# A fused Fourier-mixing and feed-forward kernel: six of seven output sums with second-level products, and a batch held in quarters

## Chip, cores and metric

The kernel runs on one core of one Trainium2 chip. The metric is the device time of one execution in microseconds. The core has five engines that each work through a queue of their own in order: TensorE (PE, with weight loads shown as PEld), VectorE (DVE), ScalarE (ACT), GpSimd (POOL) and SyncE (SP), which here issues transfers. Semaphores make an instruction of one queue wait for an instruction of another. PE writes its results into PSUM, which has 8 banks of 512 fp32 values per partition; the other tiles lie in SBUF.

## The reference

```python
def _attn_ref(x):                      # x: (8, 3008, 256) fp32
    X = np.fft.fft(x, axis=1)
    X = np.fft.fft(X, axis=2)
    return X.real.astype(np.float32)

def _moe_ref(x, w_in, w_out):          # x: (24064, 256), w_in: (256, 2048), w_out: (2048, 256)
    h = x @ w_in
    g = h * (1.0 / (1.0 + np.exp(-1.702 * h)))
    return (g @ w_out).astype(np.float32)
```

All arrays are fp32. The real part of a two-dimensional Fourier transform of each of the 8 batches goes, row by row, through two matrix products with a sigmoid-weighted activation between them.

## The kernel before

**Two pipelines in one.** The transform along the sequence (3008 = 47 x 64) is done per batch in two stages. Stage one folds the rows of `x` in the tile `xt` on GpSimd (`fold1`, 16 parts per batch), multiplies them by cosine and sine tables on PE (`mix1`, 4 times per batch, L233), copies the result back to `xt` on ACT (`mixed`) and spills it to DRAM (`spill`). Stage two reads it back (`fill`), fixes one column (`rotate`), and per block makes the tile `pq` with 32 small pairs of matmuls and four VectorE transposes (`stage2`, L354, three blocks per batch). The transform along the 256 channels is folded into the first weight matrix (`wcs`).

**Steps.** The feed-forward part runs in 384 steps: 8 batches x 3 blocks x 2 halves `hh` x 8 steps `p`. A step handles 256 hidden units (two groups of 128) for a group of 256 columns, or 226 in the second half of a first block. Eight steps with `p` from 0 to 7 are a group: they add up one output tile. The step loop (L989 to L1082) writes all engines' work out by hand, in the order in which each engine is to do it; nothing reorders it later. Extra work (folds, transforms, transfers) hangs on step numbers in the table `extra`. `paced` is a one-word transfer that holds SP's queue until a given step.

**One step t** (t from 8 on). `begin(t, 0)` and `begin(t, 1)` multiply the two parts of `pq` by `wcs` into a PSUM bank `x` (two banks, taken in turn); `middle(t)` has put a rank-one term there before, on ACT. Between the two, ACT copies twice the half-finished sum away (`doubled`). `begin(t, 1)` stands at the head of step t, `begin(t+1, 0)` in the middle of it. From the finished bank, `forward(t)` (ACT, L607) makes the activation of the forward rows, `backward(t)` (VectorE, L565) the values of the mirrored rows, and `activate_back(t)` (ACT, L614) their activation. So there are four operand tiles: A11, A12 (forward) and A21, A22 (backward).

**Seven products.** The second matrix product is done by a Strassen-Winograd scheme on these four tiles: seven products instead of eight, with sums S1 to S4 of the operands. GpSimd makes S1 and S3 (L622, L623); VectorE makes S2 and S4 for two steps at a time (L629, L630). The products of step t are issued three steps later (`LAG` = 3). Three of them (with A11, S2, S3) are plain products, 256 columns wide, into the banks `o0` and `o1` (`product`). The other four (A12, S4, A22, S1; two pairs) use a second level of the same scheme over two steps: VectorE makes four more sums (`deeper`, L651, 512 wide) and PE seven half-size products for each of the four (`small_products`, L685, 128 columns, k = 1 to 7), into the tile `low` of three banks, with k = 1 in `o1`. The weight sums for them are made once (`small_weights`).

**A group's end.** Three steps after a group's last step ACT copies two results out of PSUM (L754, L756) and VectorE adds others (L757, L758); in the step after that `combine_small` reads `low` in four additions (L786), `swap` moves halves between partitions on ACT in three copies, `combine_last` adds (L768, L804), and `turn_last` transposes the tile on VectorE in two halves, each of which is stored in DRAM by SP.

```python
            if t < n:
                backward(t)
            if t + 1 < n:
                doubled(t + 1)
            if t < n:
                activate_back(t)
                sums(t, nc.gpsimd)
```

Of the kernel before, what the change touches and what calls it, by code (L numbers as in the profile page):

```python
# [27 lines left out]
F32 = mybir.dt.float32  # L28
# [84 lines left out]
def kernel(ctx: ExitStack, tc, x, w_in, w_out, tab1, tab2, out):  # L113
# [6 lines left out]
    NCH = 8  # L120

    const = ctx.enter_context(tc.tile_pool(name="const", bufs=1, space=SB))
    xp = ctx.enter_context(tc.tile_pool(name="xp", bufs=1, space=SB))
    tp = ctx.enter_context(tc.tile_pool(name="tp", bufs=1, space=SB))
# [26 lines left out]
    o_banks = [psp.tile([128, 512], F32, tag=f"o{i}", name=f"o{i}") for i in range(2)]  # L151
    rest = psu.enter_context(tc.tile_pool(name="psu", bufs=1, space=PS))
    big = cv.tile([128, 19 * 1024], F32, tag="big", name="big")
# [13 lines left out]
    spare = ["b0", "b1", "b2", "o2", "o3", "o4"]  # L167
# [19 lines left out]
    xt = xp.tile([128, NJ, D], F32, tag="x", name="xt")  # L187
# [11 lines left out]
    def load_x(b, k):  # L199

        r, (p0, p1) = k // 2, PIECES[k % 2]
        t, src = xt[64 * r + p0:64 * r + p1], x[b].rearrange("(p j) d -> p j d", j=NB)[p0:p1]
        pairs = [4 * D, 8], [1, 2 * D]
        for lo, rows_, at in ((0, src, 2 * r), (16, Xr[b][p0:p1], 2 - 2 * r)):
            nc.sync.dma_start(out=t[:, lo:lo + 16, :].rearrange("p (i c) d -> p i (c d)", c=2),
                              in_=free(rows_, at * D, *pairs))
# [3 lines left out]
    def fold1(b, c, part, eng):  # L210

        t = xt[0:64 + NA]
        if c == 0 and part == 0:

            e, t0 = cv.tile([NA, 2, D], F32, tag="e", name="e"), xt[0:NA]
            e0[b] = e
            fwd, rev = free(t0, 1, [31 * D, 2], [1, H - 1]), free(t0, D - 1, [31 * D, 2], [-1, H - 1])
            eng.tensor_tensor(e[:, :, 1:H], fwd, rev, op=ALU.add)
            eng.tensor_copy(free(e[:], 0, [D, 2], [H, 2]), free(t0, 0, [31 * D, 2], [H, 2]))
            eng.tensor_tensor(e[:, :, H + 1:D], fwd, rev, op=ALU.subtract)  # L220

        at, up = 2 * c * D, (31 - 2 * c) * D
# [10 lines left out]
    def mix1(b, m):  # L233
# [3 lines left out]
        for i in (2 * m, 2 * m + 1):  # L237
            for r in range(2):
                for c in range(2):
                    rows, o = slice(64 * r, 64 * r + NA), ps[r][64 * c:64 * c + 64, i % 2 * D:(i % 2 + 1) * D]  # L240
                    jj, todo = 4 * i + 2 * r + c, queues.setdefault((r, c), [])
                    if jj:
                        todo.append((2, o, mat(w1, jj, rows), xt[rows, 31 - (2 * i + c), :], not todo, True))
                        continue
# [17 lines left out]
    def mixed(m, r, ps):  # L262
        nc.scalar.copy(free(xt[:], (4 * m + r) * D, [2 * D, 2], [1, D]), free(ps[:], 0, [D, 2], [1, D]))
# [73 lines left out]
    def spill(b, c, q):  # L337

        nc.sync.dma_start(out=view(Td[b], (16 * c + 4 * q) * D, [NJ * D, NM], [1, 4 * D]),
                          in_=xt[64 * c:64 * c + NM, 4 * q:4 * q + 4, :].rearrange("p q d -> p (q d)"))  # L340

    def fill(b, a0=0, a1=NG):
        if a0 == 0:
            t4t[b] = tp.tile([128, NG, D], F32, tag="t4", name="t4")
        nc.sync.dma_start(out=t4t[b][:, a0:a1, :], in_=Td[b].rearrange("(a p) d -> p a d", p=128)[:, a0:a1, :])

    def rotate(b, a0=0, a1=NG, copy=None):

        col = t4t[b][:, a0:a1, H]
        ps = bank("psr")  # L350
        halves(ps[:, 0:a1 - a0], rot, col, start=True, stop=True)
        (copy or nc.vector.tensor_copy)(col, ps[:, 0:a1 - a0])

    def stage2(b, blk):  # L354

        pq, t4 = pqp.tile([128, 2, 512], F32, tag="pq", name="pq"), t4t[b]
# [3 lines left out]
        for cs in range(2):  # L360
            for h in range(2):
                for g in range(4):
                    for u in range(NU):
                        rows, at = slice(64 * u, 64 * u + 64), cs * 256 + h * 128
                        nc.tensor.matmul(ps[u][32 * g:32 * g + 32, at:at + 128], lhsT=m[rows, cs, h * RUN:(h + 1) * RUN],  # L365
                                         rhs=t4[rows, 4 * blk:4 * blk + 4, cs * H + 32 * g:cs * H + 32 * g + 32],
# [23 lines left out]
    def paced(t):  # L390
        nc.sync.dma_start(out=Tk[t:t + 1, :], in_=big[0:1, at_left(t, A11):at_left(t, A11) + 1])
# [118 lines left out]
    LEFT, MADE, RIGHT, SUM, RES, OUT = 0, 4096, 8192, 14336, 16384, 18432  # L510
    A11, A21, S3, S2 = range(4)
    A12, S4, A22, S1 = range(4)
# [26 lines left out]
    def at_left(t, q):  # L539
        return LEFT + t % 4 * 1024 + q * 256  # L540

    def at_right(t, q):
        return RIGHT + (t // 2 % 3 * 2 + t % 2) * 1024 + q * 256

    def left(t, q, n):
        return big[:, at_left(t, q):at_left(t, q) + n]
# [3 lines left out]

    def front(t):
        at = at_left(t, A11)
        return free(big[:], at, [at_right(t, A12) - at, 2], [1, width(t)])

    def back(t):
        at = at_left(t, A21)
        return free(big[:], at, [at_right(t, A22) - at, 2], [1, width(t)])
# [51 lines left out]
    def backward(t):  # L609
        at = at_left(t, A21)  # L610
        reversed_sum(big[:, at:at + 256], at_right(t, A22) - at, gt.pop(t), xb.pop(t), width(t), ALU.subtract)

    def activate_back(t):
        nc.scalar.activation(back(t), back(t), ACTF.Gelu_apprx_sigmoid)  # L614

    def sums(t, eng):

        if not NP <= t < len(steps):
            return
        n = width(t)  # L620
        if eng is nc.gpsimd:
            eng.tensor_tensor(right(t, S1, n), left(t, A21, n), right(t, A22, n), op=ALU.add)  # L622
            eng.tensor_tensor(left(t, S3, n), left(t, A11, n), left(t, A21, n), op=ALU.subtract)  # L623
            return
        if t % 2 == 0:
            return
        a11, s2 = (free(big[:], at_left(t - 1, q), [1024, 2], [1, n]) for q in (A11, S2))
        a12, s4, s1 = (free(big[:], at_right(t - 1, q), [1024, 2], [1, n]) for q in (A12, S4, S1))
        eng.tensor_tensor(s2, s1, a11, op=ALU.subtract)  # L629
        eng.tensor_tensor(s4, a12, s2, op=ALU.subtract)  # L630
# [5 lines left out]
    def raws(t, half):  # L636

        return free(big[:], at_right(t, 0) + half * (width(t) // 2), [256, 4], [1, width(t) // 2])

    def made_sum(q, w):  # L640
        return free(big[:], SUM + 512 * q, [128, 4], [1, w])

    def deeper(t, part):
# [5 lines left out]
        for out, i0, i1, how in (((s3, a11, a21, ALU.subtract), (s1, a21, a22, ALU.add), (s2, s1, a11, ALU.subtract)),  # L649
                                 ((s4, a12, s2, ALU.subtract),))[part]:  # L650
            nc.vector.tensor_tensor(out, i0, i1, op=how)  # L651

    SPOT = {2: 0, 6: 1, 5: 2, 7: 3, 3: 4, 4: 5}

    def spot(pair_, k):
        return 256 + 128 * pair_ if k == 1 else 768 * pair_ + 128 * SPOT[k]

    def both(k, *dims):
        return free((o_banks[1] if k == 1 else pot["low"])[:], spot(0, k), [spot(1, k) - spot(0, k), 2], *dims)

    def small_products(t, ks):

        if t < 0 or not deep(t) or not steps[t][3] % 2:
            return
        p, w = steps[t][3] - 1, width(t) // 2
        for k in ks:
            for pr in range(2):
                for side in range(2):
                    op_ = 2 * pr + side
                    weights, q = ((wo, 2), (wo, 3), (wt, 2), (wt, 3))[op_]  # L670
                    y0, y1 = (weights[:, p + i, q, :] for i in range(2))
                    at = MADE + (p // 2 * 2 + pr) * 512 + side * 64
                    lhs = {1: y0[:, 0:64], 2: y1[:, 0:64], 3: y1[:, 64:128]}.get(k)
                    if lhs is None:
                        at += {5: 0, 6: 1, 7: 2, 4: 3}[k] * 128
                        lhs = big[:, at:at + 64]
                    raw_ = {1: (t - 1, 0), 2: (t, 0), 4: (t, 1)}.get(k)
                    if raw_:
                        rhs = right(raw_[0], op_, 256)[:, raw_[1] * w:raw_[1] * w + w]
                    else:  # L680
                        i0 = SUM + 512 * {5: 0, 6: 1, 7: 2, 3: 3}[k] + 128 * op_
                        rhs = big[:, i0:i0 + w]
                    first_in = p == 0 and (k, pr) in ((2, 0), (2, 1), (4, 1))
                    o = (o_banks[1] if k == 1 else pot["low"])[64 * side:64 * side + 64, spot(pr, k):spot(pr, k) + w]
                    nc.tensor.matmul(o, lhsT=lhs, rhs=rhs, start=first_in, stop=(p == NP - 2), skip_group_check=True)  # L685

    def small_weights(n):

        def y(i, at):
            return free(wot[:], (2 * n + i) * 4 * H + 2 * H + at, [NF // 2 * 4 * H, 2], [H, 2], [1, 64])  # L690

        b11, b12, b21, b22 = y(0, 0), y(0, 64), y(1, 0), y(1, 64)
        t1, t2, t3, t4 = (free(big[:], MADE + n * 1024 + q * 128, [512, 2], [64, 2], [1, 64]) for q in range(4))
        for out, i0, i1 in (t1, b12, b11), (t2, b22, t1), (t3, b22, b12), (t4, b21, t2):
            nc.vector.tensor_tensor(out, i0, i1, op=ALU.subtract)

    def product(t, lo, hi):

        p, n = steps[t][3], width(t)
        if lo == 0 and p == 0:  # L700
            for q in range(2):
                pot[q] = bank(f"po{q}", f"o{q}")
            if t >= NP:
                pot[2] = pot["low"]
            if t >= last:
                pot[3] = bank("po3", "b2")
        if t < NP:

            h = ht[t]
            plan = [(half, dh, wo[:, p, 2 * f + dh, :], h[:, half, f, :n])  # L710
# [400 lines left out]
```

## Time and profile before

| what | value |
|---|---|
| runs | 1854.57, 1854.43 and 1856.62 us; median 1854.57 |
| profiled execution | 1853.1 us from its first to its last instruction (its time by the clock of the runs is not given apart) |
| PE busy | 1836.6 us, 99% |
| VectorE busy | 1520.9 us, 82% |
| ACT busy | 1150.5 us, 62% |
| GpSimd busy | 975.2 us, 53% |
| granted TensorE clock | 0.999 |
| HBM | 64.41 MB read, 48.05 MB written, 61 GB/s |

The profile is of one execution. "Busy" is the share of the span in which an engine worked on at least one instruction, so overlapping instructions count once. The line numbers in profiles are those of the kernel that was profiled. Every fp32 matmul is recorded twice, and products come in pairs (two halves of 64 output rows), so four records make one pair.

### The profile page before, as it was taken

The page shows a single profiled execution, that of the slowest core. Times are in us where ns is not written, and L with a number is a line of the kernel's source. Part 1 is how long each engine was busy: PE and PEld are TensorE (multiplying, and loading weights), DVE is VectorE, ACT ScalarE, POOL GpSimd, SP SyncE. Part 2 cuts the span into 40 slices and gives each one's busy share as a digit, 9 for nine tenths or more (in the row PEclk, how much of TensorE's full clock was granted, in tenths as well). Part 3 has the DMA queues.
Part 4 walks back from the last instruction along what each step waited for, and adds up shares of the span by engine and source line. Part 5 has one row for each costly group of instructions (what it writes and reads, how often), then busy time and mean ns, then how long its engine had stood idle before and what let it go on. Part 6 is the DMA issues. An engine that isn't in the chain of part 4 may idle for free.

```text
span 1853.1 us, 56093 instructions
## 1 busy us (share of the span) xinstructions
PE 1836.6 (99%) x23722; PEld 1401.3 (76%) x23722; DVE 1520.9 (82%) x2222; ACT 1150.5 (62%) x2241; POOL 975.2 (53%) x1053
## 2 busy tenths in 40 slices
PE   8999999999999999999999999999999999999998
PEld 4677777777777777777777777777777777778776
DVE  6988778887798778987789878888888888878874
ACT  5666656665666666666566666666665666656663
POOL 4776446744368434773348643485445754444442
PEclk9999999999999999999999999999999999999999
DMA  8721340215012240223302132121411111100111
GB/s 280 181 61 34 85 67 19 72 52 99 19 46 48 73 81 13 52 50 90 57 13 67 43 86 52 19 75 35 103 31 23 37 46 36 31 19 13 23 19 24
DMA packets 149707, 105.31 MB, mean 57 GB/s; under 512 B 106057, under 2 KB 130665, under 8 KB 148896
## 3 DMA queue, kind: packets, MB, share of 16 engines
q1 hardware_dynamic: 146624, 99.68, 23.6%
q8 instruction: 187, 3.06, 0.7%
q10 hardware_dynamic: 2832, 2.05, 0.5%
q14 instruction: 64, 0.52, 0.1%
HBM read 64.41 MB, written 48.05 MB: 61 GB/s over the span
## 4 chain that ended last, share of the span: by engine, by line
PE 80%; DVE 9%; POOL 4%; ACT 2%; DMA 2%; issue 2%; SPq 0%; DVEq 0%; ACTq 0%; POOLq 0%
PE x L184 29%; PE o L184 22%; PE low L685 21%; PE o L685 3%; DVE big L651 3%; PE ps L255 2%; DVE big L786 2%; DVE big L565 1%; PE ps L365 1%; POOL xt L227 1%; DVE big L629 1%; POOL big L623 1%; DMA xt<-in_x_dram 1%; ACT big L607 1%; DMA Td<-big 1%
## 5 line engine op out<-in xcount | busy, mean ns | idle before, releaser
L622 POOL TENSOR_TENSOR big<-big 128x256 f32<-128x256 f32 (+1 forms) x376 | 353.0, 939 | 825.1 <-ACT big L614 691.4
L184 PE MATMUL x<-pq,wcs 128*64 128x256 f32 (+1 forms) x6016 | 768.8, 376 | 2.0 <-ACT g L604 1.4
L651 DVE TENSOR_TENSOR big<-big 128x512 f32<-128x512 f32 (+1 forms) x736 | 623.1, 861 | 23.4 <-PE low L685 4.7
L184 PE MATMUL o<-big,wo 128*64 128x256 f32 (+1 forms) x4800 | 620.8, 375 | 0.1
L184 PEld LDWEIGHTS x<-pq,wcs 128*64 128x64 f32 x6016 | 412.3, 137 | 186.0 <-issue 15.0
L184 PEld LDWEIGHTS o<-big,wo 128*64 128x64 f32 x4800 | 341.6, 137 | 148.0 <-DVE big L629 0.5
L604 ACT ACTIVATE g<-x 128x512 f32<-128x512 f32 (+1 forms) x376 | 221.6, 589 | 366.3 <-PE x L184 365.0
L565 DVE TENSOR_TENSOR big<-g,x 128x512 f32<-128x512 f32 (+2 forms) x440 | 254.1, 589 | 209.4 <-ACT big L607 209.0
L592 ACT ACTIVATE x<-nb,af 128x256 f32<-128x256 f32 (+1 forms) x752 | 352.9, 469 | 79.7 <-DVE pq L371 63.6
L685 PE MATMUL low<-big 128*64 128x128 f32 (+1 forms) x5888 | 382.8, 270 | 0.0
L685 PEld LDWEIGHTS low<-big 128*64 128x64 f32 x5888 | 337.5, 137 | 29.2
L623 POOL TENSOR_TENSOR big<-big 128x256 f32<-128x256 f32 (+1 forms) x376 | 352.6, 938 | 0.0
L607 ACT ACTIVATE big<-x 128x512 f32<-128x512 f32 (+1 forms) x376 | 219.2, 583 | 127.5 <-PE x L184 121.3
L614 ACT ACTIVATE big<-big 128x512 f32<-128x512 f32 (+1 forms) x376 | 231.9, 617 | 46.0 <-DVE big L565 44.0
L685 PE MATMUL low<-big,wo 128*64 128x128 f32 (+1 forms) x2944 | 220.4, 271 | 0.1
L685 PEld LDWEIGHTS low<-big,wo 128*64 128x64 f32 x2944 | 171.3, 137 | 4.2 <-DVE big L651 1.4
L630 DVE TENSOR_TENSOR big<-big 128x512 f32<-128x512 f32 (+1 forms) x188 | 160.8, 855 | 6.5
L629 DVE TENSOR_TENSOR big<-big 128x512 f32<-128x512 f32 (+1 forms) x188 | 137.3, 730 | 5.3 <-POOL big L622 5.3
L786 DVE TENSOR_TENSOR big<-big,low 128x512 f32<-128x512 f32 (+3 forms) x184 | 109.0, 609 | 3.5
L685 PEld LDWEIGHTS o<-big,wo 128*64 128x64 f32 x1472 | 92.2, 137 | 25.0
L685 PE MATMUL o<-big,wo 128*64 128x128 f32 (+1 forms) x1472 | 110.0, 270 | 0.0
L227 POOL TENSOR_TENSOR xt<-xt 111x510 f32<-111x510 f32 x56 | 86.0, 1535 | 4.4
(95 smaller groups left out, 966.2 us busy)
## 6 DMA issues: line engine op xcount, KB each, us to landing
out_dram<-os SPq DMA_DIRECT2D x284, 64.0 KB
t<-Td SPq DMA_DIRECT2D x22, 512.0 KB
Td<-xt SPq DMA_DIRECT2D x56, 192.0 KB
xt<-in_x_dram SPq DMA_DIRECT2D x14, 512.0 KB
xt<-Xr SPq DMA_DIRECT2D x14, 512.0 KB
nb<-Nd SPq DMA_DIRECT2D x23, 256.0 KB
out_dram<-os SPq DMA_DIRECT2D x96, 56.0 KB
Xr<-in_x_dram SPq DMA_DIRECT2D x7, 752.0 KB
```

What stands on the lines that cost most here:

```text
L184: nc.tensor.matmul(out[c0:c0 + 64], lhsT=lhs[:, c0:c0 + 64], rhs=rhs, skip_group_check=True, **how)
L565: nc.vector.tensor_tensor(free(out, at + m - 1, [by, 2], [RUN, blocks], [-1, m]), *ins, op=op)
L592: nc.scalar.activation(x[:, i * 256:i * 256 + n], nbt[b, blk][:, hh * 256:hh * 256 + n], ACTF.Copy, scale=af1[:, f:f + 1])
L604: nc.scalar.activation(two(g[:], n), two(xb[t][:], n), ACTF.Copy, scale=2.0)
L607: nc.scalar.activation(front(t), two(xb[t][:], width(t)), ACTF.Gelu_apprx_sigmoid)
L614: nc.scalar.activation(back(t), back(t), ACTF.Gelu_apprx_sigmoid)
L622: eng.tensor_tensor(right(t, S1, n), left(t, A21, n), right(t, A22, n), op=ALU.add)
L623: eng.tensor_tensor(left(t, S3, n), left(t, A11, n), left(t, A21, n), op=ALU.subtract)
L629: eng.tensor_tensor(s2, s1, a11, op=ALU.subtract)
L630: eng.tensor_tensor(s4, a12, s2, op=ALU.subtract)
L651: nc.vector.tensor_tensor(out, i0, i1, op=how)
L685: nc.tensor.matmul(o, lhsT=lhs, rhs=rhs, start=first_in, stop=(p == NP - 2), skip_group_check=True)
```

## The change

- Six of the seven operands (A12, S4, A22, S1, S2, S3: three pairs) now go through the second level; only A11 keeps a plain product. `deeper` works on 768 columns, `small_product` has three pairs, `small_weights` makes more weight sums.
- All output sums lie in one tile `low` of six PSUM banks; `o0`, `o1` and the bank `b2` are given up, so the transforms take both `x` banks. A step with a transform issues products of two steps around it, and the step after it none of its own. Products wait in a list `pending`, from which `issue(n)` takes about n ns of them.
- A21 is written back into the `x` bank (ACT), and S3 and S1 are made on VectorE from there, S2 and S4 on GpSimd.
- The batch in transformation is held in two quarters of 8 columns (`xq`, inside the tile `big`) in place of the whole `xt`; loads, folds, `mix1` and spills follow quarter by quarter, spread over a batch's steps. `t4` is held per block, and `rotate` is done per block.
- `combine`, `swap`, `combine_last` and `turn_last` are re-timed; `doubled(t+1)` stands behind `activate_back(t)`.

```diff
-    LEFT, MADE, RIGHT, SUM, RES, OUT = 0, 4096, 8192, 14336, 16384, 18432
+    LEFT, SUM, MADE, RIGHT, RES, TMP, MADE2, KEPT, OUT = 0, 1024, 4096, 8192, 17408, 18944, 19456, 21504, 23040
+    A12, S4, A22, S1, S2, S3 = range(6)
...
+    def activate_back(t, there):
+        n = width(t)
+        x = xb.pop(t)
+        a21[t] = x[:, 0:n] if there else turned_rows(t, n)
+        nc.scalar.activation(a21[t], turned_rows(t, n), ACTF.Gelu_apprx_sigmoid)
+        nc.scalar.activation(right(t, A22, n), right(t, A22, n), ACTF.Gelu_apprx_sigmoid)
+
+    def sums(t):
+        n, a = width(t), a21.pop(t)
+        nc.vector.tensor_tensor(right(t, S3, n), left(t, n), a, op=ALU.subtract)
+        nc.vector.tensor_tensor(right(t, S1, n), a, right(t, A22, n), op=ALU.add)
+        nc.gpsimd.tensor_tensor(right(t, S2, n), right(t, S1, n), left(t, n), op=ALU.subtract)
+        nc.gpsimd.tensor_tensor(right(t, S4, n), right(t, A12, n), right(t, S2, n), op=ALU.subtract)
...
     def made_sum(q, w):
-        return free(big[:], SUM + 512 * q, [128, 4], [1, w])
+        return free(big[:], SUM + 768 * q, [128, 6], [1, w])
...
+    SPOT = {1: 0, 2: 1, 6: 2, 5: 3, 7: 4, 3: 5, 4: 6}
+    PAIRS = 3
     def spot(pair_, k):
-        return 256 + 128 * pair_ if k == 1 else 768 * pair_ + 128 * SPOT[k]
+        return 256 + 384 * SPOT[k] + 128 * pair_
...
+    def units(t):
...
+        todo += [(436, product, t, *it) for it in plan(t)]
+        if t >= NP and p % 2 and deep(t):
+            now = [(222, small_product, t, k, pr) for k in (1, 2, 4, 7) for pr in range(PAIRS)]
+        if t > NP and p % 2 == 0 and deep(t - 1):
+            late = [(222, small_product, t - 1, k, pr) for k in (5, 6, 3) for pr in range(PAIRS)]
+        return late + todo + now if p == 0 else todo + late + now
...
         if deep(t):
-            nc.scalar.copy(free(big[:], RES + 1024 + 384, [512, 2], [1, n // 2]), both(1, [1, n // 2]))
+            nc.scalar.copy(free(big[:], KEPT + 384, [512, PAIRS], [1, n // 2]), both(1, [1, n // 2]))
+            return
...
+            now, after, soon = (k in special for k in (t, t - 1, t + 1))
+            if now and special[t][0] is stage2:
+                spare[:] = [f"b{(t + 1) % 2}"]
+                rotate(*special[t][1])
+            if t < n:
+                begin(t, 1)
...
+                forward(t)
+            combine(t - LAG - 1)
+            if t == NP + LAG:
+                psu.close()
+                low = ctx.enter_context(tc.tile_pool(name="low", bufs=1, space=PS))
+                pot["low"] = low.tile([128, 6 * 512], F32, tag="low", name="low")
+            if not after:
+                pending += units(t - LAG)
+            if now:
+                backward(t)
+                activate_back(t, False)
+                issue(1750)
+                deeper(t - 2, 0)
+                deeper(t - 3, 2)
+                sums(t)
+                transform(t)
+                deeper(t - 2, 1)
+                deeper(t - 3, 3)
+                pending += units(t + 1 - LAG)
+                issue(2100 if special[t][0] is stage2 else 1800)
+                begin(t + 1)
+                doubled(t + 1)
+                middle(t + 2)
+                issue(880)
+            else:
+                issue(0 if after else 1100)
+                if t + 1 < n:
+                    begin(t + 1)
+                held = [pending.pop() for _ in range(5)][::-1] if t - LAG == last else []
+                issue()
+                if t < n:
+                    backward(t)
+                    activate_back(t, True)
+                if t + 1 < n:
+                    doubled(t + 1)
+                deeper(t - 2, 0)
+                deeper(t - 3, 2)
+                if t < n:
+                    sums(t)
+                if t + 2 < n and not soon:
+                    middle(t + 2)
+                combine_small(t - LAG - 1)
+                pending += held
+                issue()
+                deeper(t - 2, 1)
+                deeper(t - 3, 3)
```

## The prediction

> **What bounds the kernel now.** I read the page's first two parts, then the busy table of one plain group of eight steps, the groups by shape, and the timeline around a group's end. The page:
> ```profile
> span 1853.1 us, 56093 instructions
> PE 1836.6 (99%) x23722; PEld 1401.3 (76%) x23722; DVE 1520.9 (82%) x2222; ACT 1150.5 (62%) x2241; POOL 975.2 (53%) x1053
> PEclk9999999999999999999999999999999999999999
> ```
> TensorE is busy 99% at full clock. The table from 203.07 to 239.47 us, eight steps without a transform (time; PE, PEld, DVE, ACT, POOL busy):
> ```profile
> 203.07:239.47 36.40, 36.40 (x508) 28.30 (x504) 29.32 (x45) 21.71 (x42) 15.43 (x16) 1.00 0.45 90
> ```
> PE never pauses, VectorE has 7 us left. The timeline where a group ends (start, length):
> ```profile
> 286.30 0.39 PE L685 MATMUL low<-big,wo 128*64 128x128 f32 x4
> 286.73 2.46 DVE L786 TENSOR_TENSOR big<-big,low 128x512 f32<-128x512 f32 x4
> 287.38 1.46 PE L184 MATMUL o<-big,wo 128*64 128x256 f32 x12
> 288.67 1.03 PE L184 MATMUL x<-pq,wcs 128*64 128x256 f32 x8
> ...
> 292.13 0.61 PE L685 MATMUL low<-big,wo 128*64 128x128 f32 x8
> 292.57 1.04 PE L685 MATMUL low<-big 128*64 128x128 f32 x16
> ```
> Two things are to be seen. Four records are one pair of halves: x12 against x8 gives 0.43 us per 256-column pair, x16 against x8 0.215 per 128-column pair (8 x 7 x (0.43 + 0.215) = 36.1, against 36.40). And VectorE reads `low` for 2.46 us from 0.04 us after its last product, while PE next writes `low` 5.4 us later: covered.
>
> The shapes that price the new work (mean ns behind the bar):
> ```profile
> L607 ACT ACTIVATE big<-x 128x512 f32<-128x512 f32 x312 | 184.7, 592 | 109.1 <-PE x L184 103.4 <-POOL big L623 3.1 <-DMA out_dram<-os 0.6
> L565 DVE TENSOR_TENSOR big<-g,x 128x512 f32<-128x512 f32 x312 | 210.7, 675 | 192.9 <-ACT big L607 192.7
> L804 DVE TENSOR_TENSOR big<-big 128x768 f32<-128x768 f32 x38 | 36.7, 966 | 3.9
> L786 DVE TENSOR_TENSOR big<-big,low 128x256 f32<-128x256 f32 x38 | 15.7, 414 | 0.0
> L754 ACT COPY big<-o 128x256 f32<-128x256 f32 x39 | 14.2, 365 | 5.7 <-PE o L184 5.7
> L592 ACT ACTIVATE x<-nb,af 128x256 f32<-128x256 f32 x624 | 295.3, 473 | 50.8 <-DVE pq L371 40.0
> ```
> The second says that `backward` waits for `forward`. How fast PE resumes after ACT:
> ```profile
> 368.00 0.60 ACT L604 ACTIVATE g<-x 128x512 f32<-128x512 f32 x1
> 368.65 0.65 PE L184 MATMUL x<-pq,wcs 128*64 128x256 f32 x4 [0.24 <-ACT g L604]
> ```
> That is 0.05 us. An engine's next start lies closer than the mean length: L604 to L614 0.50 (287.65 and 288.15), L754 to L756 0.27, the 768-wide L804 to L565 0.88.
>
> **Products.** A deep step had 7 pairs of each size; it gets 5 wide and 10.5 narrow ones. That is 2 x 0.43 - 3.5 x 0.215 = 0.11 us less, 0.86 a group; the table's 36.40 would have 0.22 for a narrow pair and 0.72. I take 0.8: for 46 groups, 8 of them 226 wide, **-36** (32 to 39). It is all on PE, so on the path. Rotating per block adds 15 pairs of tiny matmuls at 0.1 to 0.2: **+2**.
>
> **First wait at a group's end.** `low` now holds all sums. In the program as built, 46 times, in the step where p is 3 (three behind the group's last), the first product after `begin(t,1)` waits for ACT's copy of the k=1 sums, though it writes other columns. ACT must first do `forward(t)`, which waits for that same `begin`. From the first matmul of `begin`: its records end at 1.03, ACT starts 0.11 later, 0.50 to the copy of c11, 0.27 to the 384-wide copy, whose length between the 365 (256 wide) and the 592 (512 wide) is 0.48, then 0.05: 2.44. PE would have gone on at 0.86. Lost: 1.58.
>
> **Second wait.** The first of the four `combine_small` additions waits for the new group's opening product, the last of that step. The next product, after the next `begin`, waits for the last addition; every later product stands behind it in PE's queue. The product's end trails its issue by 0.17, VectorE starts 0.04 later; 0.88 + 0.88 + 0.47 + 0.97 = 3.20 (the 384-wide between the 414 and the 687 of the 256- and 512-wide L786); 0.05 to PE. `begin` covers 0.86. Lost: 0.17 + 0.04 + 3.20 + 0.05 - 0.86 = 2.60. VectorE is free by then: its `S1` ends at about 4.0 (`backward` starts at 1.77; 0.61, 0.88, 0.33, 0.41) and the opening product at 5.9 (2.44, nine narrow pairs, a `begin`, a product, 0.17).
> Together 4.18 a group, about 3.8 in the 226-wide: 38 x 4.18 + 8 x 3.8 = **+189**. Bounds by the rows: the 384-wide copy 0.37 to 0.60, the additions 2.46 (as before) to 3.9 (four of 966): 3.3 to 5.0 a group, 152 to 225; the middle, for the 768 row is the very shape.
>
> [...] The built program waits, so I count it.
>
> **Steps after a transform.** There are 50 (28 `mix1`, 22 `stage2`). The transforming step takes products of two steps, so its successor has two `begin`s and 4 (`stage2`) or 5 (`mix1`) narrow pairs: 2.58 or 2.80 us of PE. `doubled(t+1)`, for which the following `begin` waits, now stands on ACT behind both `activate_back`s, and they wait for `backward`: 1.03 + 0.11 + 0.59 + 0.03 + 0.68 + 0.03 + first activation 0.27 to 0.41 (L754, L592) + second 0.27 + doubled 0.60 + 0.05 = 3.66 to 3.80. Lost: 22 x 1.15 + 28 x 0.93 = **+51** (30 to 65). Plain steps last 4.1 to 4.8 and cover the chain. Two short stops per batch around `mix1` (0.50 and 0.24 in the timeline) fall into this: **-3** (-5 to 0).
>
> **VectorE and GpSimd.** By start to start, VectorE has per step `backward` 0.61, S3 and S1 0.33 each, two 768-wide sums 1.75, and per group 6.5 of combining: 3.83 a step against 3.1 before. S1 and S3 take A21 from PSUM: like L565 they should not be slowed by GpSimd, while sums with two SBUF inputs are (L651 averages 857 for 512 columns, about 680 without GpSimd beside). At up to 0.6 of that VectorE needs 4.4 of PE's 4.45: cover is thin without the waits, but with them a step averages over 5 us. **0** (up to +10); late sums would stop PE in the short steps first. GpSimd's two sums run behind S1 and are needed a step later: nothing.
>
> **Transfers.** Loads go from 56 DMAs to 224, markers from 63 to 91, on SP's queue between stores and spills. That queue waited 885 us for `os`, so it has room; 32 added issues per batch at 0.3 to 1.6 lie beside PE. A quarter is asked for two steps (9 us) before its first fold. If it came late, that fold, and GpSimd's sums queued behind it, would wait, and PE after a step's slack. **0** (0 to +10). Spills and fills keep five steps to `stage2`.
>
> **Head.** `small_weights` issues 8 VectorE additions for 4, about 1.1 us in each of four steps (PE was short of work there: steps of 5.8 and 7.1); and `low` takes over the o-banks at step 11, behind two transposes: **+4** (0 to 8). The tail is one loop pass longer, with no PE work in it.
>
> **Sum**: 1853 - 36 + 2 + 189 + 51 - 3 + 4 = 2060 of span; the runs' median lies 1.5 above the span: **2062**, 11% slower. 0.2% is about what a measurement of this kernel can tell from no change.
>
> **Rivals.**
> *PE stays the bound*: the waits are met early, and only the products count. 1853 - 36 + 2 + 4 + 1.5 = 1825. For it: TensorE's 99%. Against: the additions alone last 3.2 us behind 0.86 of cover; it decides where PE idles under 0.8 us a group; I count 5.2.
> *Only the steps after a transform stall*: the group's end is covered by something that I count as serial, as it was before (5.4 us against 2.46). 1825 + 48 = 1873. Against: both waits stand between neighbours in PE's queue.
> *VectorE too*: PE idles as forecast and VectorE, kept waiting for the opening product, cannot catch up, so the following steps each lose some 0.6 to GpSimd: up to 46 x 2 = 92 more, 2150. Against: 34 us of VectorE in groups of 42.
> *The clock falls* in the new pauses. No row here shows it: the longest pause in mid-kernel is 0.51 and the clock 0.999.
> [...]
>
> **Numbers.** Forecast 85%, from 2020 (waits and after-steps at their lower ends, 37 + 21 less, not both in full) to 2105 (the upper ends in part). Faster rival 4%, the 1873 one 5%, the two above 6%. The 2 in 10 that may be left out are the rivals and the forecast's own tails, so the range stays 2020 to 2105. Faster 0.05, same 0.01, slower 0.94.
>
> **What would show it.** Right: PE's busy share near 88%; 46 pauses of about 1.4 before a narrow `low` product released by ACT's 384-wide copy, 46 of about 2.4 before a wide one released by `combine_small`; 50 of about 1 before an `x` matmul released by `doubled`; PE's busy sum some 30 us lower. Wrong: `low` products that start while those additions run, VectorE busy over 95%, or a clock below 0.95.

## The result, and the profile after

The changed kernel takes 2250.05 us (median of 4 runs, 2237.58 to 2256.38) against 1854.57: 1.2119 times the time before [1.2083, 1.2156]. The forecast was 2062 (2020 to 2105). The sign was right; the loss is 396 us where 207 were forecast. The profiled execution has a span of 2254.6 us and a mean TensorE clock of 0.966.

The page of the changed kernel: span, then busy time, share and instructions by engine, and the clock by slice:

```profile
span 2254.6 us, 61518 instructions
PE 1940.9 (86%) x25990; PEld 1508.5 (67%) x25990; DVE 1665.0 (74%) x2629; ACT 1245.4 (55%) x2617; POOL 1005.8 (45%) x1053
PEclk9999999999999999999999999999999999999999
```

TensorE stands 314 us, and its busy share comes close to the one that I named (86 for 88%). That is chance: the forecast had some 257 us of standing and 1803 us of work, and both are too low. TensorE's busy time is 104 us more than before, though the products became less work. For the larger part that is the sign of slower matmuls, which a row of forty slices rounded to tenths does not show. The waits, summed by the waiting engine and its releaser (total us, times, longest):

```profile
PE low L185 <- DVE big L802: 121.1, 46, 3.5
PE low L681 <- ACT big L773: 64.0, 46, 1.7
PE x L185 <- ACT g L602: 58.1, 74, 3.1
PE ps L255 <- DVE big L563: 29.3, 26, 2.0
PE psr L185 <- DVE big L625: 10.2, 15, 1.0
PE ps L364 <- DVE t L351: 6.3, 14, 0.6
```

The first three are forecast: both waits at `low`, and `x` behind `doubled` (L602). The last three, about 50 us with what lies beside them, stand inside transforms and were forecast at nothing. A group's end, as the timeline of the changed kernel shows it (start, length, what ended the idle time before):

```profile
526.67 0.60 ACT L605 ACTIVATE big<-x 128x512 f32<-128x512 f32 x1 [0.90 <-PE x L185]
527.16 0.37 ACT L771 COPY big<-low 128x256 f32<-128x256 f32 x1
527.41 0.50 ACT L773 COPY big<-low 128x384 f32<-128x384 f32 x1
527.96 1.31 PE L681 MATMUL low<-big 128*64 128x128 f32 x20 [1.40 <-ACT big L773]
...
531.49 3.40 DVE L802 TENSOR_TENSOR big<-big,low 128x768 f32<-128x768 f32 x4 [1.97 <-PE low L185]
...
534.94 0.65 PE L185 MATMUL low<-big,wo 128*64 128x256 f32 x4 [2.64 <-DVE big L802]
536.08 1.84 PE L185 MATMUL x<-pq,wcs 128*64 128x256 f32 x8
```

The pauses of 1.40 and 2.64 are the two that were worked out. The last line was not: eight `x` matmuls of 1.03 us take 1.84, for the clock stands at 0.50 from 536.16 us on; the twelve 128-wide ones that follow take 1.50, against 0.82 at 530.19. Two stretches around a transform show it plainly (window; its length; PE, PEld, DVE, ACT, POOL busy; clock; DMA share, GB/s):

```profile
505.50:508.90 3.40, 1.61 (x24) 0.99 (x20) 3.33 (x5) 0.00 (x0) 1.92 (x2) 0.99 0.00 0
508.90:515.70 6.80, 6.54 (x46) 4.57 (x48) 4.72 (x7) 2.78 (x6) 2.70 (x2) 0.50 0.13 23
```

In the first stretch TensorE is busy 1.61 of 3.40 us, with no pause over 2.04; in the 6.8 us that follow it works almost throughout and the clock stands at 0.50. The trace has 41 such half-clock stretches, 153.7 us together, so some 77 us of TensorE's time, half of that, are lost (5.4 and 3 in the kernel before). About 25 follow the second pause at a group's end, ten lie in steps that transform.

### The profile page after: what moved, and what is told of

It is laid out like the page before. It is cut to its first block, busy times and chain, and to the rows that moved or that the text cites. A ratio compares the mean times of both kernels' runs of the same rounds, so it can differ in the third digit from the quotient of the medians.

```text
span 2254.6 us, 61518 instructions
## 1 busy us (share of the span) xinstructions
PE 1940.9 (86%) x25990; PEld 1508.5 (67%) x25990; DVE 1665.0 (74%) x2629; ACT 1245.4 (55%) x2617; POOL 1005.8 (45%) x1053
## 3 DMA queue, kind: packets, MB, share of 16 engines
q10 hardware_dynamic: 2832, 2.05, 0.4%
## 5 line engine op out<-in xcount | busy, mean ns | idle before, releaser
L648 DVE TENSOR_TENSOR big<-big 128x768 f32<-128x768 f32 (+1 forms) x736 | 733.7, 997 | 0.0
L681 PE MATMUL low<-big 128*64 128x128 f32 (+1 forms) x8832 | 588.9, 276 | 64.0 <-ACT big L773 64.0
L681 PEld LDWEIGHTS low<-big 128*64 128x64 f32 x8832 | 516.6, 140 | 144.1 <-ACT big L773 84.5
L563 DVE TENSOR_TENSOR big<-g,x 128x512 f32<-128x512 f32 (+2 forms) x440 | 257.4, 597 | 463.5 <-ACT big L605 461.2
L681 PE MATMUL low<-big,wo 128*64 128x128 f32 (+1 forms) x6624 | 460.8, 278 | 0.0
L681 PEld LDWEIGHTS low<-big,wo 128*64 128x64 f32 x6624 | 400.8, 141 | 55.9 <-issue 12.4
L185 PE MATMUL low<-big,wo 128*64 128x256 f32 (+1 forms) x1696 | 255.1, 390 | 122.6 <-DVE big L802 121.1
L616 ACT ACTIVATE x<-big 128x256 f32<-128x256 f32 (+1 forms) x326 | 125.1, 384 | 361.6 <-DVE big L563 358.3
L602 ACT ACTIVATE g<-x 128x512 f32<-128x512 f32 (+1 forms) x376 | 217.2, 578 | 172.4 <-PE x L185 171.2
L185 PEld LDWEIGHTS low<-big,wo 128*64 128x64 f32 x1696 | 117.0, 140 | 183.1 <-DVE big L802 141.7
L802 DVE TENSOR_TENSOR big<-big,low 128x768 f32<-128x768 f32 (+2 forms) x184 | 151.1, 838 | 89.7 <-PE low L185 86.3
L617 ACT ACTIVATE big<-big 128x256 f32<-128x256 f32 (+1 forms) x376 | 149.0, 396 | 0.0
L624 DVE TENSOR_TENSOR big<-big,x 128x256 f32<-128x256 f32 (+1 forms) x326 | 132.7, 407 | 3.7 <-ACT x L616 3.7
L625 DVE TENSOR_TENSOR big<-x,big 128x256 f32<-128x256 f32 (+1 forms) x326 | 133.8, 410 | 0.0
L616 ACT ACTIVATE big<-big 128x256 f32<-128x256 f32 (+1 forms) x50 | 20.7, 414 | 106.3 <-DVE big L563 106.3
```

The lines of the kernel that those rows point to most:

```text
L185: nc.tensor.matmul(out[c0:c0 + 64], lhsT=lhs[:, c0:c0 + 64], rhs=rhs, skip_group_check=True, **how)
L563: nc.vector.tensor_tensor(free(out, at + m - 1, [by, 2], [RUN, blocks], [-1, m]), *ins, op=op)
L602: nc.scalar.activation(two(g[:], n), two(xb[t][:], n), ACTF.Copy, scale=2.0)
L616: nc.scalar.activation(a21[t], turned_rows(t, n), ACTF.Gelu_apprx_sigmoid)
L617: nc.scalar.activation(right(t, A22, n), right(t, A22, n), ACTF.Gelu_apprx_sigmoid)
L681: nc.tensor.matmul(pot["low"][64 * side:64 * side + 64, at:at + w], lhsT=lhs, rhs=rhs, start=first_in, stop=(p == NP - 2), skip_group_chec ...
```

## The experiments

Each time is the median of 4 runs; the ratio, with its interval, is to the kernel before, run on the same chip. The kernel before took 1854.6 to 1856.5 us on these chips, so the times of different experiments can be compared; the changed kernel's own four runs spread over 19 us. Pauses are TensorE's idle times of over 0.1 us, from 80 us on, in the profiled run, summed by the tile that it writes next: `x`, `low`, and `ps` and `psr` inside transforms.

**The order on ScalarE, turned back.**

```diff
                     backward(t)
-                    activate_back(t, True)
                 if t + 1 < n:
                     doubled(t + 1)
+                if t < n:
+                    activate_back(t, True)
```

> The changed kernel with one order turned back: in steps without a transform, ScalarE issues doubled(t+1) ahead of activate_back(t), as the kernel before had it. The changed kernel's trace has 62.3 us of TensorE pauses before an x matmul (82 of them), put down mostly to ScalarE's g; the term of the forecast for them was 51. Theory (the order on ScalarE makes them): these pauses fall under 15 us, PE's other pauses stay as they are, and the time falls by 45 to 60 us, to about 2195 of 2250. Rival (the order is not the cause: backward, or the product before it, is late anyway): the time stays within 10 us and the pauses move to the next product.

Measured: 2295.94 us, 1.2376 [1.2347, 1.2405], 46 slower. Theory and rival both fell. The `x` pauses did drop, from 62 to 21 us, but the others grew: `low` from 187 to 210, transforms from 50 to 92; half clock from 154 to 201 us. A group's end of this kernel:

```profile
535.73 0.60 ACT L602 ACTIVATE g<-x 128x512 f32<-128x512 f32 x1 [2.33 <-PE x L185]
536.23 0.38 ACT L616 ACTIVATE x<-big 128x256 f32<-128x256 f32 x1
536.64 0.42 DVE L624 TENSOR_TENSOR big<-big,x 128x256 f32<-128x256 f32 x1 [2.21 <-ACT x L616]
537.31 3.39 DVE L802 TENSOR_TENSOR big<-big,low 128x768 f32<-128x768 f32 x4
540.75 0.65 PE L185 MATMUL low<-big,wo 128*64 128x256 f32 x4 [2.96 <-DVE big L802]
```

ScalarE now stands at `doubled` (L602) for TensorE, with `activate_back` (L616) behind it; VectorE waits 2.21 for that, and the additions, for which TensorE waits, start later: 2.96 in place of 2.64. The larger growth, 42 us, lies inside transforms. There too TensorE waits for VectorE's `backward` (L563), and that comes later. The transform whose matmuls wait 2.04 us in the changed kernel (shown further down) waits here:

```profile
515.44 1.97 PE L255 MATMUL ps<-big,w 47*64 47x256 f32 x12 [2.97 <-DVE big L563]
```

**The second wait, then both, taken away.** The additions of `combine_small` read SBUF (`kept` is a region of `big`); in the second kernel the two copies do too.

```diff
-        for out, i0, i1 in ((res(RES, KEPT - RES), res(KEPT + 384, 0), both(2, [384, 2], [1, w])),
+        for out, i0, i1 in ((res(RES, KEPT - RES), res(KEPT + 384, 0), kept(2, [384, 2], [1, w])),
...
-        nc.scalar.copy(c11, pot[0][:, 0:n])
+        nc.scalar.copy(c11, big[:, MADE:MADE + n] if deep(t) else pot[0][:, 0:n])
```

> The changed kernel, in which the four additions of combine_small read a fixed region of SBUF in place of low; left out is the use of the sums that low holds. The additions stay, of the same shapes; nothing but the copies at the first wait now reads low at a group's end. The second wait goes: 46 pauses, 122.6 us of TensorE idle time. Theory A (the wait and the clock): idle time falls by 110 to 130 us, and of the 41 stretches at half clock the 30 or so that follow the second pause go too, another 45 to 60 us of slow matmuls: 2250 - 170 = about 2080 (2065 to 2095). Theory B (idle time alone; the half clock comes from elsewhere and stays): 2250 - 125 = about 2125, with about 40 half-clock stretches left. Theory C (VectorE is behind, and its lateness comes back at the next wait): less than 60 us gained.

> As the run before it in this list, and in addition the copies of c11 and of the k=1 sums by ScalarE read SBUF at a group's end: nothing reads low there (left out: all use of the deep sums). Both waits go. Against the run with the second wait alone taken away: theory A, the first wait was a cost of its own, and 46 x 1.39 = 64 us go, to about 2015. Rival: the pause only moves to the x matmuls behind it, for ScalarE's forward ends the same step, and less than 25 us go. If the forecast's other terms hold, what is left over the 1825 of my first rival is then the steps after a transform (62), the transform waits (50) and what clock is lost there.

Measured: 2167.33 us, 1.168 [1.1652, 1.1707], and 2167.91 us, 1.1677 [1.1657, 1.1696]. Two pauses worth 187 us of TensorE gave 82, less than theories A and B and more than C, and the first of them gave nothing, as its rival had it: the `x` pauses grew from 62 to 126 and 178 us. Half clock fell from 154 to 57 us and, without the first wait, rose to 131 again. The kernel without either wait, at a group's end:

```profile
2046.84 4.23 DVE L805 TENSOR_TENSOR big<-big 128x768 f32<-128x768 f32 x4
...
2051.85 0.68 DVE L563 TENSOR_TENSOR big<-g,x 128x512 f32<-128x512 f32 x1
2052.56 0.39 ACT L616 ACTIVATE x<-big 128x256 f32<-128x256 f32 x1 [3.77 <-DVE big L563]
...
2053.19 0.58 ACT L602 ACTIVATE g<-x 128x512 f32<-128x512 f32 x1
2053.82 1.08 PE L185 MATMUL x<-pq,wcs 128*64 128x256 f32 x8 [1.82 <-ACT g L602]
```

The additions hold up `backward` (L563) behind them, that ScalarE, that TensorE. The edit also lengthens them, 3.40 to 4.23 us, for both inputs now lie in SBUF; so these two runs understate the waits.

**The clock by itself.** Products with zero weights fill the two pauses.

```diff
+                for lag, pairs in ((1, 3), (2, 5)):
+                    if t + 1 < n and group_end(t - LAG - lag):
+                        idle(t + 1, pairs)
                 issue(0 if after else 1100)
```

> The changed kernel with zero-weight products in the two pauses at each group's end: 3 pairs of 64-row halves, 256 columns wide, where the first pause is (1.3 of 1.39 us), 5 pairs where the second is (2.15 of 2.64 us). They add zero to the x bank just written, so nothing of the result changes, and TensorE has 46 x 3.4 = 157 us more to do. Theory (the clock follows how busy TensorE was in the stretch before): of the 41 half-clock stretches 153.7 us long in all, the 30 behind the second pause go, and the time FALLS by 35 to 60 us though work is added, to about 2200. Rival (the clock is no cause; pauses are just time): the products fit into the pauses or overrun them, and the time stays or rises by up to 40 us. The mean clock of the profiled run tells: 0.966 now; by the theory 0.985 or more.

Measured: 2207.96 us, 1.1898 [1.188, 1.1916], 42 faster with 101 us more on TensorE (PE busy 2041.8 for 1940.9). Half clock fell from 153.7 to 36.3 us, which gives back 59, and the mean clock rose from 0.966 to 0.992, as the theory had it; the rest went into overrunning the pauses. The rival, that pauses are just time, falls.

**VectorE's additions, late sums and the order, left out one upon another.** From the kernel without reads of `low`:

```diff
-                combine_small(t - LAG - 1)
+                if t < 4 * NP:
+                    combine_small(t - LAG - 1)
...
-            combine_last(t - LAG - 5, 0)
+            if t < 4 * NP:
+                combine_last(t - LAG - 5, 0)
```

> As the kernel in which nothing reads low at a group's end, and in addition the four additions of combine_small are left out behind all but the first two deep groups (their sums are not made). Theory (VectorE's 3.4 us in one piece set the step they stand in, whatever PE waits for by name: backward, S3 and S1 of the next step are queued behind them, and with backward, activate_back, doubled and the next begin): without them the step that lasted 7.1 us falls to 4.8 or less, x pauses of 178 us to under 90, and with them half of the half-clock stretches: 44 x 2.3 = 100 and 30 to 50 of clock off 2167, so about 2030 (2000 to 2070). Rival (VectorE has slack there, and the pauses come from ScalarE's order alone): less than 30 us.

> As the run before it in this list, and part 0 of combine_last (two 256-wide additions and one 512-wide) is left out too behind all but the first two deep groups: these stand on VectorE in the last step of a group of eight, ahead of the transforms that follow. Theory: what remains of TensorE's waits inside a transform (28 us before ps in stage one's matmuls, 8 before psr) falls below 15, and the half-clock stretches in those steps go: 25 to 50 us less. Rival (a transform's matmuls wait for that step's own backward, whatever stands before): less than 10 us.

> As the run before it in this list, with doubled(t+1) ahead of activate_back(t) on ScalarE, the order of the kernel before, as in the first experiment, where it cost 46 us. Theory (that order cost there because activate_back, S3, S1 and the additions behind them on VectorE, which PE waited for, came later; with nobody waiting for VectorE it gains): the x pauses nearly go, and the time is within 40 us of the 1825 that the products alone would give, plus the 1.15 us of each stage2: 1825 to 1890. Rival (the order is bad by itself): no faster than the run before it.

Measured: 2020.01 us, 1.0888 [1.0872, 1.0904]; 1949.68, 1.0505 [1.0489, 1.0521]; 1945.27, 1.049 [1.0468, 1.0511]. The additions are worth 148 us (at their 4.23), the late sums 70; the 4 of the order are less than the runs' own spread of 8. The first theory held. The second held in direction and was short of the size: with the sums gone, the pauses before `ps` in stage one fell from 30 to 7 us and half clock from 66 to 23, while those before `psr` stayed at 12.6. The third failed: 1945 lies above its 1825 to 1890. The order took `x` pauses from 65 to 25 us, and inside transforms they grew from 19 to 43.

**Late sums one step later**, in the changed kernel itself.

```diff
-            combine_last(t - LAG - 5, 0)
-            combine_last(t - LAG - 6, 1)
+            combine_last(t - LAG - 6, 0)
+            combine_last(t - LAG - 7, 1)
```

(`turn_last` moves with it.)

> The changed kernel with combine_last and the two transposes behind it one step later each: VectorE then gets part 0 behind the work of the transforming step instead of ahead of it; the result is the same. Theory: TensorE's waits inside transforms (30 us before ps, 10 before psr, 10 before the row's ps) fall to under 20, and of the nine half-clock stretches in those steps most go: 2250 falls by 30 to 60 us. Rival (VectorE's order there only moves the wait): within 15 us of 2250.

Measured: 2189.05 us, 1.1793 [1.1776, 1.1811], 61 faster, at the upper end. The pauses inside transforms fell from 50 to 17 us, and half clock from 153.7 to 102.2, so some 26 of the 61 came through the clock. What it moves out of the way, in the changed kernel's trace:

```profile
505.97 1.81 DVE L820 TENSOR_TENSOR big<-big 128x256 f32<-128x256 f32 x2
507.81 0.69 DVE L784 TENSOR_TENSOR big<-big 128x512 f32<-128x512 f32 x1
508.42 0.68 DVE L563 TENSOR_TENSOR big<-g,x 128x512 f32<-128x512 f32 x1
509.16 1.97 PE L255 MATMUL ps<-big,w 47*64 47x256 f32 x12 [2.04 <-DVE big L563]
```

2.5 us of part 0 stand ahead of `backward`, which must read the `x` bank before the transform may write it. The stretch at half clock shown above begins there.

**Banks of the transforms' own.** From the kernel of 1945: `low` gets 4 banks, and the transforms the 2 that this frees; then the same with the changed kernel's order.

```diff
-        spare[:] = [f"b{(t + 1) % 2}", f"b{t % 2}"]
+        spare[:] = ["c0", "c1"] if own else [f"b{(t + 1) % 2}", f"b{t % 2}"]
...
-                pot["low"] = low.tile([128, 6 * 512], F32, tag="low", name="low")
+                pot["low"] = low.tile([128, 4 * 512], F32, tag="low", name="low")
```

> The kernel without combining sums and with doubled first (1945), in which low has 4 banks in place of 6 (the deep sums of three of seven products then share columns with others, so what they hold is left out of use) and the transforms write the 2 banks won, in place of the two x banks. Theory (what is left over the 1825 of the products alone is the transforms' waits for x: a transform's matmuls wait for backward to read the bank, and the x work behind them waits for the transform's readers): TensorE's idle time of 70 us falls under 20 and the time to 1825 to 1850. Rival (a transform's own copies, transposes and turned row make its waits, in whatever bank): not under 1920.

> As the run before it in this list, but with the changed kernel's order on ScalarE (doubled behind activate_back). It tells what the 62 us of pauses before x come from. My forecast's step (the order, 50 times 1 us): 50 us of them stay and this kernel is 40 to 60 us slower than the run before it. Rival (the banks: the order matters only because the transform held them): within 12 us of it.

Measured: 1889.54 us, 1.0181 [1.0166, 1.0196], and 1920.61, 1.0349 [1.0334, 1.0365]. The waits for `x`, first in the one, then in the other:

```profile
PE x L187 <- ACT x L592: 25.1, 49, 2.8
```

```profile
PE x L187 <- ACT g L604: 65.4, 86, 3.2
```

The banks are worth 56 and 29 us, and with them the order is worth 31: between theory (40 to 60) and rival (12). The first theory's 1850 was missed: 25 us of pauses remain behind `middle` (L592); what delays it was not followed. No run gives the transforms banks of their own in a kernel that makes all sums.

**The waits follow the tile.** `low` as two tiles, at the same columns: banks 0 and 1, banks 2 to 5. Then with the late sums a step later, too.

```diff
-                pot["low"] = low.tile([128, 6 * 512], F32, tag="low", name="low")
+                pot["low"] = [low.tile([128, b * 512], F32, tag=f"low{b}", name=f"low{b}") for b in (2, 4)]
...
-        for out, i0, i1 in ((res(RES, KEPT - RES), res(KEPT + 384, 0), both(2, [384, 2], [1, w])),
+        for out, i0, i1 in ((res(RES), res(KEPT + 384), both(2, [1, w])), (res(KEPT), res(KEPT + 384), both(6, [1, w])),
```

> The changed kernel with low as two tiles at the same columns: banks 0 and 1 (A11, k=1, k=2), banks 2 to 5 (the rest); the first addition of combine_small is two of 384 columns; the result is the same. Theory (the waits follow the tile, not the columns): the first pause, 64 us, falls under 15 us, the second, 123 us, to under 80, for only the narrow products of k=4 and 7 wait for all the additions. As taking both waits away altogether gave 82 us because VectorE's additions stayed, the time falls by 50 to 85 us, to 2165 to 2200. Rival (the reads and products do exclude each other): 2250.

> As the run before it in this list, and combine_last with its transposes one step later, which alone gave 61 us; the result is the same. If the two causes are separate the gains add: 2110 to 2140. If both gains came by the same route (VectorE's lateness at the transforms) less than 20 us come on top of the first.

Measured: 2120.06 us, 1.1424 [1.1405, 1.1443], and 2070.27, 1.1153 [1.1137, 1.117]. The pauses before products into `low` fell from 187 to 7 us and half clock from 154 to 33, at the price of `x` pauses of 140: 130 us, more than the 50 to 85 expected. Two things differ from the kernels that read SBUF: the additions keep their length (3.46 us a group, 4.22 there), and less half clock is left (33 us for 57 and 131). The second edit gave 50 more, so the gains nearly add.

**The order once more, and the additions' own order.** From the kernel of 2070, with the edit of the first experiment; then with the addition that reads bank 1 made last.

> The kernel of 2070 (low in two tiles, combine_last a step later) with doubled(t+1) ahead of activate_back(t); the result is the same. This order cost 46 us in the changed kernel and gained 31 where nobody waits for VectorE and the transforms have banks of their own. Theory (in the changed kernel it cost because TensorE stood at low's two waits for work that the order puts later; without those waits it uncouples doubled from VectorE, which stands 3.5 us in the additions): the 142 us of x pauses fall by 40 or more, and the time to 1990 to 2040. Rival (the order is bad while transforms hold the x banks): 2070 or slower.

> As the run before it in this list, and the additions of combine_small that read banks 2 to 5 come ahead of the one that reads bank 1, so that they need not wait for the new group's opening product, which writes bank 0; the result is the same. Theory (by its 13 us of waits of VectorE for that product in the kernel of 2070): 5 to 15 us less than the run before it. Rival (products of k=1 and 2 then wait for the last addition): 10 to 60 us more.

Measured: 2057.87 us, 1.1083 [1.1067, 1.11], and 2164.5, 1.1656 [1.1627, 1.1685]. Without the waits at `low` the order no longer costs, it gains 12 us; the theory's direction held, its size did not: `x` pauses fell from 142 to 73 us, but transforms' waits rose from 21 to 46 and `low`'s from 8.5 to 16.5. The last run is a miss that shows the second wait and the clock together; its rival was right, and too low (107 us):

```profile
1210.18 3.44 DVE L808 TENSOR_TENSOR big<-big,low 128x339 f32<-128x339 f32 x5
1213.68 1.04 PE L185 MATMUL low<-big,wo 128*64 128x256 f32 x4 [3.52 <-DVE big L808]
1214.49 1.50 PE L685 MATMUL low<-big,wo 128*64 128x128 f32 x12
```

If the addition that reads the tile of banks 0 and 1 comes last, the next A11 product waits for all five: 146 us of pauses before `low`, 45 stretches at half clock.

No kernel here beats the one before; the best that still makes all sums takes 2057.87.

## Why the prediction was right and wrong

The forecast had the waits at `low` and the steps after a transform, and as pauses they came nearly as worked out. The step that failed is the one that put the rest at nothing: VectorE at 0 by an average over a step, the transforms' waits for the `x` banks with no term at all, and the clock as a rival, judged by the length of single pauses. The trace has 74 us of lost clock and 50 us of waits inside transforms there.

- **Products, -36**: right in direction, some 14 us too large by the records. In the kernel with own banks TensorE is busy 1834.0; less half of 24.8 us at half clock and 62 pauses' ends of 0.17 it is 1811. The kernel before, treated alike, has 1831, so the work became some 20 us less, where 36 - 2 = 34 were forecast.
- **The two waits, +189**: right as pauses. The first is 46 x 1.39 by the trace (1.41 forecast), the second 46 x 2.63 (2.43 forecast: the four additions took 3.40 for the 3.20 worked out). They follow the tile, as the built program had them: with the tile cut, they went, while VectorE read banks 2 to 5 during products into banks 0 and 1. But as prices they were not 189. Read as time to be had back, they give 130, and that with the clock that they cost; VectorE's additions then show as pauses before `x`. The prediction treated the additions as a cost only through `low`.
- **Steps after a transform, +51**: right as pauses. Of the 58 us behind `doubled`, 50 pauses with 45 us stand 7 to 11 us behind a transform's last matmul, and 24 with 13 us stand elsewhere. The order that it named does make them (62 us fell to 21 when it was turned back), but it is no price by itself: turning it back is worth -46, 4, 12 or 31 us, depending on who else is late.
- **VectorE, 0**: failed. I compared its work per step (3.83) with the step's length, an average, and said that late sums would stop TensorE in the short steps. What counted were two places where it works 2.5 and 3.4 us in one piece, ahead of `backward`: part 0 of `combine_last` before a transform, and `combine_small`. The first alone costs 61 us, 26 of them through the clock; the second is hidden behind the second wait while that lasts, and is worth 148 us (at 4.23) where both waits are gone.
- **The x banks** were in the text of the change, and no term of the sum had them: a transform that writes them waits for `backward`. With banks of their own, in the kernels without the sums, they gain 29 to 56 us.
- **The clock, a rival**: failed as judged, and is the largest term that was missing: 77 us lost by the trace, 42 by the run that filled the pauses and still had work to add. I dismissed it because its longest pause, about 2.4 us, seemed too short; that such a pause leaves the clock alone was my estimate, and no run shows it. The trace has 25 windows lost at group ends and 20 elsewhere. What counted in these runs is not one pause but all standing in a window. All half-clock stretches of a run begin on one grid of 3413 ns, from the first to the last. I laid windows on that grid and took TensorE's busy share in each from the records. Seven of the kernels (the changed one and those of 2295.94, 2167.91, 2207.96, 2189.05, 2070.27 and 2164.5 us) give, from 60 us on, for windows at full clock without a transform's matmuls:

| TensorE busy in the window | windows | next at half clock |
|---|---|---|
| under 0.4 | 152 | 152 |
| 0.4 to 0.5 | 64 | 10 |
| over 0.5 | 3252 | 0 |

All sixteen kernels together give 175 of 175, 15 of 74 and 0 of 7395. So 2.05 us of standing in one window were enough here. A pause of 2.64 that falls at random on the grid leaves a window with that in 0.77 + 2 x 0.59 of 3.41 cases, 57% or 26 of 46; some 25 were seen. With 1.7 us each, half a window, the term could have been 44, before the transforms'.

The length of a single pause does not tell the stretches: 38 of the changed kernel's 41 follow windows whose longest pause is 2.74 us or less (the others follow pauses of 3.15 and 3.49 us, and the kernel's last product). Nor did a window have to be without work, for windows with up to 0.4 of it were enough.

- **Transfers 0, head +4**: right. The one DMA that TensorE waits for costs 2.2 us, at the start; TensorE's idle time that is not in pauses from 80 us on is 15.4 us against 11.8.

Against the forecast's span of 2060.5 the trace has 194 more. The clock is 74 of it, the transforms' waits 50, `x` 11, the second wait 11, the ends of pauses not counted about 15. Some 30 us of TensorE's busy time are left over; the smaller saving on products may be half of them, the rest stays unassigned. The 61 of the late sums are no further term: they lie almost wholly within the clock and the transforms' waits.

## What to carry to other kernels

Before pricing a pause, ask what it does to the clock: add up TensorE's idle time per window (3413 ns in these runs, where 2.05 us of standing were enough), not the longest pause. And when a wait is to be removed, follow the engine that made it: if the work that TensorE waited for stays in one piece in front of something TensorE needs a step later, the wait returns there, as 187 us of pauses that gave 82. An order is worth what the engines behind it make of it; the same two lines cost 46 us in one kernel and gained 31 in another.

## What the runs showed of the hardware that was not expected

In the changed kernel the half clock comes in whole windows of 3413 ns (37 stretches of one, 4 of two) on a grid that runs on from the first to the last, and it goes with a share: by the table above it followed every window under 0.4 busy and none over 0.5. Windows that hold stage one's matmuls (47 rows in place of 128) were followed by half clock up to a busy share of 0.75: 19 of 88 between 0.5 and 0.8 in the seven kernels. Windows with stage two's alone (64 rows) never were, 0 of 91. Why, no run here tells.

The same additions took 951 ns with one input in PSUM and 1173 with both in SBUF (128 x 768, mean of 114; first the changed kernel, then the kernel with the second wait taken away):

```profile
L802 DVE TENSOR_TENSOR big<-big,low 128x768 f32<-128x768 f32 x114 | 108.4, 951 | 75.4 <-PE low L185 74.1
```

```profile
L805 DVE TENSOR_TENSOR big<-big 128x768 f32<-128x768 f32 x114 | 133.7, 1173 | 1.3
```

The difference goes with GpSimd's work: with both inputs in SBUF, in the second of these kernels, the 26 additions with no GpSimd instruction beside them took 946 ns on average, the 7 with GpSimd at work throughout 1508; with one input in PSUM, in the changed kernel, it was 950 and 954. So in these kernels moving an operand out of PSUM, to free a bank or a wait, was paid on VectorE as far as GpSimd worked beside it.
